# Retention and a tanh-shrink MLP on one core: who issues the transposing transfer's store, and seven products for one half block more

## The chip, the core and the metric

The kernel runs on one core of a Trainium2 chip. TensorE multiplies matrices (the profile calls it PE, and its weight loads PEld), VectorE (DVE), ScalarE (ACT) and GpSimd (POOL) work on elements, SyncE (SP) issues transfers. The metric is the device time of one launch in microseconds; before the change it is 741.86 us, the median of three runs (741.45 to 742.57). The profiled execution spans 740.2 us.

## The reference

```python
# attention: q, k, v are (4, 8, 768, 64)
gamma = 1.0 - 2.0 ** (-5.0 - np.arange(H))
for t in range(S):
    state = gamma * state + np.einsum('bhd,bhe->bhde', k[:, :, t], v[:, :, t])
    y[:, :, t] = scale * np.einsum('bhd,bhde->bhe', q[:, :, t], state)
x = y.transpose(0, 2, 1, 3).reshape(B * S, H * D)      # (3072, 512)
# MLP: w_in (512, 2048), w_out (2048, 512)
h = x @ w_in
out = (h - np.tanh(h)) @ w_out
```

## The kernel before

The 3072 rows are handled in 24 *chunks* of 128 (attention) and in 12 *half blocks* of 256 (MLP). The retention is computed chunk by chunk: scores of a chunk (masked products of k and q), plain sums of outer products of k and v (the state), and outputs. For the scores, k and q are needed transposed. The first eight chunks are transposed on TensorE, the other sixteen by a transfer: ScalarE splits the words of k and scaled q into 16-bit halves (`apart`), one transfer stores them in DRAM (`rows`), and a second, transposing transfer reads them back as `kqT`.

```python
def turn_by_dma(ci):
    apart = mid.tile([P, 2, 2, H * D], U16, tag="apart", name=f"apart_{ci}", bufs=1)
    for which in range(2):
        words = loaded[ci][which].rearrange("p h d -> p (h d)").bitcast(U16)
        nc.scalar.copy(out=apart[:, :, which],                                   # L277
                       in_=words.rearrange("p (n two) -> p two n", two=2))
    rows = dram.tile([P, 2, 2 * H * D], U16, tag="rows", name=f"rows_{ci}")
    nc.sync.dma_start(out=rows, in_=apart.rearrange("p two i n -> p two (i n)"))  # L280
    sides[ci] = mid.tile([P, 2, NP, P], F32, tag="kqT", name=f"kqT_{ci}")
    nc.sync.dma_start_transpose(                                                  # L282
        out=sides[ci].rearrange("p i n t -> p (i n) t").bitcast(U16),
        in_=rows.rearrange("p two n -> (p two) n"),
    )
```

`products(ci)` multiplies first k with v (L302, the plain sums) and then the two sides of `kqT` (L308, the scores), into the two PSUM banks with the tag "t".

The weights arrive as 64-bit floats and are converted on the chip, one tile of 128 x 512 after the other: two ScalarE operations (L176, L177), four of VectorE (L185 to L191), two of GpSimd (L199, L203). `load_weights` on SyncE's queue (L153, L158) fills one of three `raw` buffers and waits until the buffer is free.

The MLP runs in *steps*: in each, `up` makes 256 columns of h for one half block (8 matmuls of 128x256, L420), ScalarE and VectorE turn h into g = h - tanh(h), and two steps later `down` multiplies that g with the output weights. An ordinary `down` is 4 matmuls of 128x512 (L468). From half block FAST on, the 2x2 block product is done with seven products in place of eight (the Strassen-Winograd form): 7 matmuls of 128x256 (L579), for which GpSimd makes four sums of each g (L544 to L547) and, once, 16 differences of weights (L535). At the end of such a half block one ScalarE copy and seven VectorE operations put its results together.

Each matmul of the code stands as two records in the profile, so `up` is x16, an ordinary `down` x8, and seven products x14.

```python
FAST = 6
...
def fast_weights(k, at):
    if not room:
        ...                            # buffers of "raw", "head", "low", "power"
        late = xp.tile([P, 4, 2, TH], F32, tag="xT", name="fast_x")
        room.extend(late[:, i] for i in range(4))
    ...
    nc.gpsimd.tensor_tensor(t, a, b, op=ALU.subtract)                             # L535
...
def fast_banks(n):
    if not spare:
        t = banks("t", "fast_t")
        whole = y_banks.rearrange("p two r n t -> p r two n t")
        spare.append([t[:, 0], t[:, 1], whole[:, 0].rearrange("p two n t -> p (two n t)"),
                      bank("o", "fast_o"), bank("o", "fast_o")])
        spare.append(whole[:, 1].rearrange("p two n t -> p (two n t)"))
    five, sixth = spare
    first, second, third = five[:3]
    spare[0] = five[3:] + [first, second, third]
    ...
```

A half block takes three of the five banks in turn and half of the sixth. `y_banks` are the outputs' two banks, "o" those of the ordinary `down`.

The main loop, steps 8 to 95. Steps with a chunk (`ci`) are 9, 11, 13 and so on to 45; `ci` is 5 in step 9 and 20 in step 39. Half blocks 0 to 3 share the first 32 steps; half block 4 has steps 32 to 39, half block 5 steps 40 to 47, and each later one eight more.

```python
with_chunk = {BEGUN + 2 * i + 1: FIRST - 3 + i for i in range(NCH - FIRST + 3)}
with_weights = {BEGUN: [12, 13]}
for i in range(14, NW):
    with_weights[i - 5] = [i]
with_fast = {4 * NM // 2 + 1 + i: (i % 4, i // 4) for i in range(2 * PAIRS)}

for s in range(BEGUN, len(steps)):
    n, m2, first, last = steps[s]
    ci = with_chunk.get(s)
    if ci is not None:
        if ci + 3 < NCH:
            scale(ci + 3, 0, nc.gpsimd)          # q, L240
            scale(ci + 3, 1, nc.gpsimd)          # v, L240
        if ci >= FIRST:
            outputs_rest(ci)
            keep_x(ci)
        if FIRST <= ci + 2 < NCH:
            products(ci + 2)                     # L302, L308
            mask(ci + 2)
            state(ci + 2)
        load_chunk(ci + 4)                       # k, q, v, L233
        if FIRST <= ci + 1 < NCH - 1:
            outputs(ci + 1)
            see(ci + 1)
    for i in with_weights.get(s, []):
        convert(i)
        load_weights(i + 3)
    for i in range(2):
        up(n, m2, i)
    ...
    if ci is not None and ci + 3 < NCH:
        turn_by_dma(ci + 3)
    waiting.append(steps[s])
    shrink_begin(n, m2)
    shrink_factors(n, m2)
    shrink_multiply(n, m2)
    downs(LAG)                                   # LAG = 2
    shrink_end(n, m2)
    if n >= FAST:
        fast_sums(n, m2)
    if s in with_fast:
        fast_weights(*with_fast[s])
downs(0)
```

Of the kernel before, what the change touches and what calls it, by code (L numbers as in the profile page):

```python
# [32 lines left out]
def kernel(  # L33
# [24 lines left out]
    nc = tc.nc  # L58
# [6 lines left out]
    NM = DF // P  # L65
    CPB = S // P
    NCH = NT // P
# [19 lines left out]
    def bank(tag, name):  # L87
        return ps.tile([P, BANK], F32, tag=tag, name=name)

    def banks(tag, name):  # L90

        return ps.tile([P, 2, BANK], F32, tag=tag, name=name, bufs=1)
# [4 lines left out]
    at = [0]  # L97
# [22 lines left out]
    NW = 2 * NM  # L120
# [84 lines left out]
    def convert(i):  # L205
        convert_begin(i)
        convert_bits(i)
        convert_end(i, nc.gpsimd)
# [17 lines left out]
    def load_chunk(ci):  # L226
        if ci >= NCH:
            return
        b, j = divmod(ci, CPB)
        loaded[ci] = []  # L230
        for nm, src in (("k", k), ("q", q), ("v", v)):
            t = inp.tile([P, H, D], F32, tag=nm, name=f"{nm}_{ci}", bufs=4 if nm == "v" else 2)
            nc.sync.dma_start(out=t, in_=src[b, :, ts(j, P), :].rearrange("h p d -> p h d"))  # L233
            loaded[ci].append(t)

    def scale(ci, which, engine):
        if ci >= NCH:
            return
        t, g = loaded[ci][1 + which], (gq, gv)[which]
        engine.tensor_tensor(t, t, g[:, ts(ci % CPB, H)][:, :, None].to_broadcast([P, H, D]),  # L240
                             op=ALU.mult)
# [29 lines left out]
# [6 lines that stand above are left out]
            nc.scalar.copy(out=apart[:, :, which],  # L277
                           in_=words.rearrange("p (n two) -> p two n", two=2))
        rows = dram.tile([P, 2, 2 * H * D], U16, tag="rows", name=f"rows_{ci}")
        nc.sync.dma_start(out=rows, in_=apart.rearrange("p two i n -> p two (i n)"))  # L280
        sides[ci] = mid.tile([P, 2, NP, P], F32, tag="kqT", name=f"kqT_{ci}")
        nc.sync.dma_start_transpose(  # L282
            out=sides[ci].rearrange("p i n t -> p (i n) t").bitcast(U16),
            in_=rows.rearrange("p two n -> (p two) n"),
        )
# [26 lines left out]
    def mask(ci):  # L312
        halves = scores[ci]
        m = mid.tile([P, 2, NP, D], F32, tag="a", name=f"a_{ci}")
        nc.vector.tensor_tensor(m, halves[:, :, 0],
                                causal[:, None, None, :].to_broadcast([P, 2, NP, D]),
                                op=ALU.mult)
        masked[ci] = m
# [18 lines left out]
    y_banks = banks("y", "y").rearrange("p r (two n t) -> p two r n t", two=2, n=2)  # L337
# [44 lines left out]
    def see(ci):  # L382
        y = y_banks[:, ci % 2]
        for col in range(2):
            for r in range(2):
                nc.scalar.copy(out=seen[ds(D * col, D), r : r + 1],  # L386
                               in_=y[ds(D * col, D), r, 1, ds(D * ((ci + r + col) % 2), 1)])

    def outputs_rest(ci):
        halfway.pop(ci)(False)  # L390
        loaded.pop(ci)

    def keep_x(ci):
        n, nj = divmod(ci, BLK)
        if nj == 0:
            xT[n] = xp.tile([P, NP, BLK * P], F32, tag="xT", name=f"xT_{n}")

        half = xT[n][:, :, ts(nj // 2, TH)].rearrange("p (n r) t -> p r n t", r=2)
        y = y_banks[:, ci % 2][:, :: 1 - 2 * (ci % 2)]
        for odd in range(2):  # L400
            nc.scalar.copy(out=half[:, :, :, ds(P * odd + D * (nj % 2), D)],
                           in_=y[:, :, :, odd::2])
# [103 lines left out]

    FAST = 6
    PAIRS = NM // 2  # L510
    room = []
    t_of = {}
# [1 line left out]
    def quarter(i, c, at):  # L514
        return w2[:, i::2, ts(c, TH)][:, ds(2 * at, 2)]

    def fast_weights(k, at):

        if not room:
            for _ in range(3):  # L520
                raw = stage.tile([P, 2, 2, TH], F32, tag="raw", name="fast_raw", bufs=3)
                room.extend(raw[:, i] for i in range(2))
            for tag in ("head", "low", "power"):
                room.extend(stage.tile([P, 2, TH], F32, tag=tag, name=f"fast_{tag}")
                            for _ in range(2))
            late = xp.tile([P, 4, 2, TH], F32, tag="xT", name="fast_x")
            room.extend(late[:, i] for i in range(4))
        t = t_of[k, at] = room[PAIRS // 2 * k + at]
        a, b = (
            (quarter(0, 1, at), quarter(0, 0, at)),  # L530
            (quarter(1, 1, at), t_of.get((0, at))),
            (quarter(1, 1, at), quarter(0, 1, at)),
            (t_of.get((1, at)), quarter(1, 0, at)),
        )[k]
        nc.gpsimd.tensor_tensor(t, a, b, op=ALU.subtract)  # L535
# [13 lines left out]

    spare = []
    accs = {}

    def fast_banks(n):
        if not spare:
            t = banks("t", "fast_t")
            whole = y_banks.rearrange("p two r n t -> p r two n t")
            spare.append([t[:, 0], t[:, 1], whole[:, 0].rearrange("p two n t -> p (two n t)"),
                          bank("o", "fast_o"), bank("o", "fast_o")])  # L560
            spare.append(whole[:, 1].rearrange("p two n t -> p (two n t)"))
        five, sixth = spare
        first, second, third = five[:3]
        spare[0] = five[3:] + [first, second, third]
        acc = {1: first, 2: first, 5: second, 7: second, 3: third, 4: third, 6: sixth}
        right = {2: 1, 7: 1, 4: 1, 6: n % 2}
        accs[n] = {k: b[:, ts(right.get(k, 0), TH)] for k, b in acc.items()}

    def fast_down(n, m2, first, last):
        if first:  # L570
            fast_banks(n)
        left = fast_g.pop((n, m2))
        for k in (1, 2, 4, 6, 7, 5, 3):
            right = (
                w2[:, 2 * m2, :TH], w2[:, 2 * m2 + 1, :TH], w2[:, 2 * m2 + 1, TH:],
                *(t_of[x, m2 // 2][:, m2 % 2] for x in (3, 0, 1, 2)),
            )[k - 1]

            nc.tensor.matmul(accs[n][k], left[k - 1], right, start=first and k in (1, 6, 7, 4),  # L579
                             stop=last, skip_group_check=True)  # L580
# [28 lines left out]
    def downs(lag):  # L609
        while len(waiting) > lag:  # L610
            tile_ = waiting.pop(0)
            if tile_[0] >= FAST:
                fast_down(*tile_)
# [60 lines left out]


    FIRST = 8
    with_chunk = {BEGUN + 2 * i + 1: FIRST - 3 + i for i in range(NCH - FIRST + 3)}
    with_weights = {BEGUN: [12, 13]}
    for i in range(14, NW):
        with_weights[i - 5] = [i]  # L680
    with_fast = {4 * NM // 2 + 1 + i: (i % 4, i // 4) for i in range(2 * PAIRS)}

    for s in range(BEGUN, len(steps)):
        n, m2, first, last = steps[s]
        ci = with_chunk.get(s)
        if ci is not None:
            if ci + 3 < NCH:
                scale(ci + 3, 0, nc.gpsimd)
                scale(ci + 3, 1, nc.gpsimd)
            if ci >= FIRST:  # L690
                outputs_rest(ci)
                keep_x(ci)
            if FIRST <= ci + 2 < NCH:
                products(ci + 2)
                mask(ci + 2)
                state(ci + 2)
            load_chunk(ci + 4)
            if FIRST <= ci + 1 < NCH - 1:
                outputs(ci + 1)
                see(ci + 1)  # L700
# [5 lines that stand above are left out]
        if ci == NCH - 2:  # L706
            outputs(ci + 1)
            see(ci + 1)
        if ci is not None and ci + 3 < NCH:
            turn_by_dma(ci + 3)  # L710
        waiting.append(steps[s])
        shrink_begin(n, m2)
        shrink_factors(n, m2)
        shrink_multiply(n, m2)
        downs(LAG)
        shrink_end(n, m2)
        if n >= FAST:
            fast_sums(n, m2)
        if s in with_fast:
            fast_weights(*with_fast[s])  # L720
    downs(0)


# [52 lines left out]
```

## Time and profile before

| | us |
|---|---|
| median of three runs | 741.86 |
| span of the profiled execution | 740.2 |
| TensorE, `up` (L420), 1536 records | 351.6 |
| TensorE, ordinary `down` (L468), 384 records | 173.0 |
| TensorE waiting for `kqT` before L308 | 3.44, once |
| store `rows<-apart`, issue to landing, least / median / most | 2.9 / 3.8 / 5.4 |
| transposing transfer `kqT<-rows`, issue to landing, the same | 4.1 / 4.2 / 4.7 |

The page gives the busy time of each engine, the chain of work that ended last, the costliest groups of instructions and the transfers. In a list of waits a line names who waited, for what, how long in all, how often and the longest. In a timeline a line has the start, the duration, the engine, the line of the kernel, the operation with its output and inputs, the count, and in brackets the idle time before it with what ended it. The duration of a matmul record reaches beyond the start of the next, as matmuls are pipelined; what a group costs is read from start to start. "Granted clock" is the share of TensorE's full clock.

### The profile page before, as it was taken

How to read it: one execution, taken by the hardware profiler on the slowest of the kernel's cores; microseconds unless marked ns; L12 is line 12 of the kernel's file. 1: busy time of each engine (PE TensorE's matmuls, PEld its weight loads, DVE VectorE, ACT ScalarE, POOL GpSimd, SP SyncE). 2: the span in 40 equal slices, each digit the busy share in tenths (PEclk: the TensorE clock that was granted, in tenths of full speed). 3: DMA queues.
4: the chain of work that ended last, by engine and by line, in shares of the span. 5: the costliest groups of instructions: out<-in, count | busy, mean ns of one | idle time of the engine just before them, and what ended most of it. 6: DMA issues, size and time to landing. Idle time of an engine off the chain costs nothing.

```text
span 740.2 us, 14746 instructions
## 1 busy us (share of the span) xinstructions
PE 723.9 (98%) x5758; PEld 560.5 (76%) x5758; DVE 532.3 (72%) x843; ACT 390.0 (53%) x749; POOL 231.0 (31%) x316
## 2 busy tenths in 40 slices
PE   8899998999999999999999999999999999999996
PEld 7686665676677667667666688888888888888885
DVE  4989988898889767666455666676676766766764
ACT  4477565766767654655453444444444444444441
POOL 0565435444454412227000032222222232222221
PEclk9999999999999999999999999999999999999999
DMA  9863428676766556544200000000000000000000
GB/s 205 220 186 86 129 71 195 166 196 168 184 182 158 138 131 167 147 100 101 59 30 1 0 30 0 2 29 1 0 29 1 29 2 1 28 1 1 29 1 28
DMA packets 125396, 59.81 MB, mean 81 GB/s; under 512 B 109840, under 2 KB 118160, under 8 KB 125328
## 3 DMA queue, kind: packets, MB, share of 16 engines
q1 hardware_dynamic: 125184, 58.73, 30.8%
q8 instruction: 45, 0.74, 0.4%
q10 hardware_dynamic: 144, 0.15, 0.1%
q14 instruction: 23, 0.19, 0.1%
HBM read 35.80 MB, written 14.68 MB: 68 GB/s over the span
## 4 chain that ended last, share of the span: by engine, by line
PE 95%; DMA 2%; DVE 1%; SPq 1%; ACT 0%; issue 0%; DVEq 0%; ACTq 0%
PE h L420 45%; PE o L468 22%; PE fast_t L579 7%; PE y L579 6%; PE fast_o L579 6%; PE y L356 3%; PE s L302 1%; PE s L308 1%; PE kqTp L254 1%; PE kqTp L216 1%; DMA raw<-in_moe_w_in_dram 1%; DMA k<-in_k_dram 1%; SPq L233 1%; DMA kqT<-rows 1%; SPq L158 0%; DVE power L191 0%
## 5 line engine op out<-in xcount | busy, mean ns | idle before, releaser
L420 PE MATMUL h<-xT,w 128*128 128x256 f32 x1536 | 351.6, 382 | 1.1 <-DVE w L203 1.1
L420 PEld LDWEIGHTS h<-xT,w 128*128 128x128 f32 x1536 | 290.9, 191 | 53.1 <-issue 12.9
L429 ACT ACTIVATE u<-h 128x512 f32<-128x512 f32 x96 | 57.3, 597 | 269.4 <-PE h L420 269.1
L445 DVE TENSOR_TENSOR th<-h,th 128x512 f32<-128x512 f32 x96 | 66.2, 690 | 149.7 <-ACT th L430 149.7
L468 PE MATMUL o<-w,g 128*128 128x512 f32 x384 | 173.0, 593 | 0.0
L468 PEld LDWEIGHTS o<-w,g 128*128 128x128 f32 x384 | 72.6, 190 | 71.4 <-issue 67.9
L544 POOL TENSOR_TENSOR s<-g 128x128 f32<-128x128 f32 x48 | 21.8, 454 | 292.2 <-DVE g L459 214.3
L459 DVE COPY_PREDICATED g<-large,th 128x512 f32<-128x512 int32 x96 | 73.7, 768 | 10.2 <-DVE g L458 0.9
L448 DVE SCALAR_TENSOR_TENSOR h<-q,h 128x512 f32<-128x512 f32 x96 | 66.8, 696 | 10.4 <-DVE h L446 0.5
L454 DVE SCALAR_TENSOR_TENSOR h<-q,h 128x512 f32<-128x512 f32 x96 | 66.6, 694 | 8.6 <-DVE h L448 0.5
L199 POOL TENSOR_TENSOR low<-low,power 128x512 f32<-128x512 f32 x30 | 38.4, 1280 | 108.8 <-DVE power L191 75.2
L458 DVE TENSOR_TENSOR g<-h,u 128x512 f32<-128x512 f32 x96 | 66.3, 691 | 6.4
L437 ACT ACTIVATE q<-u,tab 128x512 f32<-128x512 f32 x96 | 69.4, 723 | 0.0
L438 ACT ACTIVATE q<-u,tab 128x512 f32<-128x512 f32 x96 | 69.1, 720 | 0.0
L439 ACT ACTIVATE large<-u,tab 128x512 f32<-128x512 f32 x96 | 68.7, 716 | 0.0
L446 DVE SCALAR_TENSOR_TENSOR h<-u,h 128x512 f32<-128x512 f32 x96 | 65.8, 685 | 0.0
L430 ACT ACTIVATE th<-h 128x512 f32<-128x512 f32 x96 | 56.8, 592 | 0.0
L240 POOL TENSOR_TENSOR q<-q,tab 128x512 f32<-128x512 f32 x22 | 24.0, 1090 | 94.0 <-DMA q<-in_q_dram 74.7
L203 POOL TENSOR_TENSOR w<-low,head 128x512 f32<-128x512 f32 x30 | 38.6, 1285 | 2.4
L356 PEld LDWEIGHTS y<-a,v 64*64 64x64 f32 x768 | 15.9, 134 | 15.3 <-ACT large L439 11.4
L240 POOL TENSOR_TENSOR v<-v,tab 128x512 f32<-128x512 f32 x22 | 27.1, 1231 | 0.1
L386 ACT COPY seen<-y 64x1 f32<-64x1 f32 x96 | 10.1, 154 | 28.3 <-PE y L356 27.9
(110 smaller groups left out, 820.8 us busy)
## 6 DMA issues: line engine op xcount, KB each, us to landing
rows<-apart SPq DMA_DIRECT2D x16, 512.0 KB, 3.8
k<-in_k_dram SPq DMA_DIRECT2D x24, 256.0 KB, 4.2
q<-in_q_dram SPq DMA_DIRECT2D x24, 256.0 KB, 4.8
v<-in_v_dram SPq DMA_DIRECT2D x24, 256.0 KB, 5.1
raw<-in_moe_w_out_dram SPq DMA_DIRECT2D x12, 512.0 KB, 4.2
out_dram<-sum SPq DMA_DIRECT2D x24, 256.0 KB, 2.3
raw<-in_moe_w_in_dram SPq DMA_DIRECT2D x14, 256.0 KB, 4.2
raw<-in_moe_w_in_dram SPq DMA_DIRECT2D x28, 128.0 KB, 4.1
```

Of the source, the lines that this page charges most:

```text
L420: nc.tensor.matmul(hp, w1[:, c, ts(2 * m2 + i, P)], xT[n // 2][:, c, ts(n % 2, TH)], start=(i == 0 and c == 0), stop=(c == NC - 1), skip_g ...
L437: nc.scalar.activation(q0, u, AF.Square, bias=bias0)
L438: nc.scalar.activation(q1, u, AF.Square, bias=bias1, scale=math.sqrt(A))
L439: nc.scalar.activation(large, u, AF.Relu, bias=bias_m)
L445: nc.vector.tensor_tensor(th, hp, th, op=ALU.subtract)
L446: nc.vector.scalar_tensor_tensor(hp, in0=u, scalar=R, in1=hp, op0=ALU.subtract, op1=ALU.mult, reverse0=True)
L448: nc.vector.scalar_tensor_tensor(hp, in0=q0, scalar=C0, in1=hp, op0=ALU.add, op1=ALU.mult)
L454: nc.vector.scalar_tensor_tensor(hp, in0=q1, scalar=A * C1, in1=hp, op0=ALU.add, op1=ALU.mult)
L458: nc.vector.tensor_tensor(flat, hp, u, op=ALU.mult)
L459: nc.vector.copy_predicated(flat, large.bitcast(I32), th)
L468: nc.tensor.matmul(o_p[j], gT[n, m2][:, i, ts(j, P)], w2[:, 2 * m2 + i], start=(first and i == 0), stop=(last and i == 1))
L579: nc.tensor.matmul(accs[n][k], left[k - 1], right, start=first and k in (1, 6, 7, 4), stop=last, skip_group_check=True)
```

## The change

The store of `apart` goes from SyncE's queue to ScalarE's, so that it needn't queue behind SyncE's other transfers. The scaling of a chunk's q and v is written at the end of the step before, and `turn_by_dma` ahead of the weights' conversion and loads and ahead of `up` instead of after it. FAST becomes 5, so that half block 5 gets its seven products too. As the outputs' banks are still in use when it starts, the order of the banks changes: the scores' two banks and one "o" bank come first, the other "o" bank is the sixth. The weights' differences are made two in a step from step 28 on instead of one in a step from step 33, and those that need the late buffer come last.

```diff
-        nc.sync.dma_start(out=rows, in_=apart.rearrange("p two i n -> p two (i n)"))
+        nc.scalar.dma_start(out=rows, in_=apart.rearrange("p two i n -> p two (i n)"))
...
-    FAST = 6
+    FAST = 5
...
+        if k == 3 and at == 0:
             late = xp.tile([P, 4, 2, TH], F32, tag="xT", name="fast_x")
...
-            whole = y_banks.rearrange("p two r n t -> p r two n t")
-            spare.append([t[:, 0], t[:, 1], whole[:, 0].rearrange("p two n t -> p (two n t)"),
-                          bank("o", "fast_o"), bank("o", "fast_o")])
-            spare.append(whole[:, 1].rearrange("p two n t -> p (two n t)"))
+            whole = y_banks.rearrange("p two r n t -> p r (two n t)")
+            o = [bank("o", "fast_o") for _ in range(2)]
+            spare.append([t[:, 0], t[:, 1], o[0], whole[:, 0], whole[:, 1]])
+            spare.append(o[1])
...
+    LAST_WEIGHTS = NW - 6
...
-    with_fast = {4 * NM // 2 + 1 + i: (i % 4, i // 4) for i in range(2 * PAIRS)}
+    fast_parts = [(k, at) for at in range(PAIRS // 2) for k in range(3)]
+    fast_parts += [(3, at) for at in range(PAIRS // 2)]
...
-            if ci + 3 < NCH:
-                scale(ci + 3, 0, nc.gpsimd)
-                scale(ci + 3, 1, nc.gpsimd)
...
             load_chunk(ci + 4)
+            if ci + 3 < NCH:
+                turn_by_dma(ci + 3)
...
-        if ci is not None and ci + 3 < NCH:
-            turn_by_dma(ci + 3)
...
-        if s in with_fast:
-            fast_weights(*with_fast[s])
+        if s + 1 in with_chunk:
+            for which in range(2):
+                scale(with_chunk[s + 1] + 3, which, nc.gpsimd)
+        if s > LAST_WEIGHTS + 1:
+            for _ in range(min(2, len(fast_parts))):
+                fast_weights(*fast_parts.pop(0))
```

## The prediction

> **What bounds the kernel now.** I read the page from the top: busy times first, then the chain that ended last.
>
> ```profile
> PE 723.9 (98%) x5758; PEld 560.5 (76%) x5758; DVE 532.3 (72%) x843; ACT 390.0 (53%) x749; POOL 231.0 (31%) x316
> ...
> PE 95%; DMA 2%; DVE 1%; SPq 1%; ACT 0%; issue 0%; DVEq 0%; ACTq 0%
> ```
>
> TensorE (PE) holds 95% of the chain. So only two kinds of gain exist: less work on TensorE, or a hole in its work closed. The idle times of the other engines cost nothing by themselves.
>
> Next, the list of waits (columns: engine and line that waited, what it waited for, total us, times, longest us). The largest of TensorE's own is this one:
>
> ```profile
> PE s L308 <- DMA kqT<-rows: 3.4, 1, 3.4
> ```
>
> It happens once. The timeline of TensorE around it (start us, duration us, engine, line, operation, count) shows where:
>
> ```profile
> 119.26 0.69 PE L302 MATMUL s<-v,k 64*64 64x64 f32 x32
> 123.40 0.69 PE L308 MATMUL s<-kqT 64*64 64x64 f32 x32 [3.44 <-DMA kqT<-rows]
> 124.02 5.41 PE L420 MATMUL h<-xT,w 128*128 128x256 f32 x16
> ```
>
> This is step 11 of the main loop, the scores of chunk 8, the first chunk turned by a transfer. Its plain sums (L302) run at 119.26, and then TensorE waits until 123.40 for `kqT`. The third line is the hidden half of the cost: the 16 up-projection matmuls that follow take 5.34 us from start to start in the chain of waits in order of time, where every other such group takes 3.45. The table by stretches says why (columns from the left: stretch, length, busy of PE, PEld, DVE, ACT, POOL, then the granted clock):
>
> ```profile
> 112.45:115.90 3.45, 3.45 (x17) 3.04 (x17) 3.28 (x6) 3.06 (x6) 1.78 (x2) 1.00 0.66 158
> 124.02:127.60 3.58, 3.58 (x15) 2.93 (x10) 3.44 (x8) 1.04 (x1) 1.44 (x1) 0.55 1.21 218
> ```
>
> The clock after the hole is 0.55, before it 1.00. So the hole costs 3.44 + (5.34 - 3.45) = 5.33 us.
>
> After 140 us TensorE never waits again: with chunks two steps take 16.06 us throughout (starts at 141.54, 157.60, 173.66 in the chain), without chunks one step takes this:
>
> ```profile
> 402.59:409.48 6.89, 6.89 (x26) 4.56 (x25) 4.12 (x6) 2.91 (x5) 0.00 (x0) 1.00 0.01 2
> 409.48:416.36 6.88, 6.88 (x25) 4.56 (x24) 4.13 (x6) 2.91 (x5) 0.00 (x0) 1.00 0.00 0
> 436.61:443.09 6.48, 6.48 (x32) 5.70 (x31) 4.13 (x7) 2.92 (x6) 1.74 (x4) 1.00 0.01 3
> 443.09:449.56 6.47, 6.47 (x31) 5.70 (x30) 4.12 (x7) 2.90 (x6) 1.73 (x4) 1.00 0.00 0
> ```
>
> The first two are steps with the ordinary down-projection, the last two with seven products. TensorE is full in all four; VectorE, ScalarE and GpSimd have over 2 us to spare.
>
> Why is the transfer late? The issues on SyncE's queue, then ScalarE's copies:
>
> ```profile
> 113.50 1.68 SPq L158 DMA_DIRECT2D raw<-in_moe_w_in_dram  x3
> 115.28 0.54 SPq L280 DMA_DIRECT2D rows<-apart  x1
> 119.07 1.95 SPq L282 DMA_TRANSPOSE kqT<-rows  x1
> ```
>
> ```profile
> 110.52 1.05 ACT L277 COPY apart<-q 128x1024 uint16<-128x1024 uint16 x1 [2.59 <-POOL q L240]
> ```
>
> `apart` is complete at 111.57, but the store goes out at 115.28, because SyncE first has to issue weight loads that wait for a free `raw` buffer (VectorE's L189 at 112.74). The store lands 3.79 us later, when the transposing transfer starts; that lands 4.28 us later, at 123.35.
>
> **What the Trainium skill says.** "DMA: Bandwidth & Descriptors", section "Anatomy of one DMA — SWDGE (gpsimd) path": transfers don't wait on semaphores, the issuing sequencer does, before dispatch. The trace agrees: 3.71 us from 111.57 to 115.28 behind another transfer's wait. The same page, "Issuing engines are not separate DMA queues": starting transfers from several engines saves only the sequencer's time. So I credit the move with that 3.71 us and not with faster landing; no run yet shows a ScalarE store here. "TensorE: Matmul & The Clock Gate", section "What's actually happening": an idle window of about 3.4 us halves the clock. The trace shows 0.55 after a hole of 3.44 us. "SBUF — State Buffer", section "SBUF: two separate sides": VectorE and GpSimd share a port pair, and one fully blocks the other. I read L187's 1.39 us at 103.19, beside GpSimd's L199 and L203, against its usual 0.43, as that.
>
> **The change part by part.**
>
> (a) *Seven products for half block 5.* Eight steps lose 4 matmuls of 128x512 (8 records) and gain 7 of 128x256 (14 records). From the table: (6.89 + 6.88)/2 = 6.885 us against (6.48 + 6.47)/2 = 6.475. That is 0.41 a step, **3.3 us** for eight. It lies wholly on the path, as TensorE is full there. Beside it GpSimd gets 32 more sums of 0.455 us (14.6 us) in steps 40 to 47, where it is idle (73.4 us idle before 425.72). VectorE gets 7 combining operations of about 0.42 us instead of one copy of 0.69; half blocks 6 to 11 do the same without TensorE waiting.
>
> (b) *Banks.* Half block 5 starts in step 42, when the outputs' banks are in use until step 45. The new order gives it the scores' two banks and two `o` banks, last read in step 41; `up` of step 42 (3.45 us) lies between. I count 0.
>
> (c) *The 16 weight differences two per step from step 28.* Each takes 1.27 to 1.52 us, so 2.5 to 3 us of GpSimd in a step of 6.9 to 9.2. Before, the last was computed at 427.49, too late for half block 5, which starts at about 376. Count: 0.
>
> (d) *The store on ScalarE, and the order.* On GpSimd the scaling keeps its place behind the weights of the step before and ahead of its own step's, so it isn't really sooner for chunk 8: q is scaled at 109.45 either way. The copy of q ends at 111.57, and I start the store at 111.65. Its landing took 2.9 to 5.4 us; with three loads just ahead (issued 108.11 to 111.15) I take 4.5, so 116.15. SyncE is free, as the weight loads now come after. Plus 4.28: `kqT` lands at 120.4, against a need at 119.95. The hole shrinks from 3.44 to about 0.5 us. That should leave the clock alone: early in the kernel a wait of 1.05 us (before 25.12) kept it at 1.00, while one of 2.17 us (before 31.31) was followed by 0.50. Gain 5.33 - 0.5 = **4.8 us**.
>
> (e) *What it delays.* ScalarE now does both copies (2.1 us) and an issue (I take 0.4, SyncE's median) ahead of the two conversion operations (1.4 us) and the activations. In step 9 these start near 113.4 instead of 111.47. VectorE's chain then runs about 1.1 us later, and so do weight tile 15 (done 122.98 before, now near 124.2; needed at 124.8) and chunk 9's scaling. I work chunk 9 on: copy of q done at 126.2, store landed at 130.8, turned at 135.1; TensorE wants it at about 135.3, since it is early by 5 us. Both fit with tenths to spare. I charge **0.3 us**.
>
> (f) The 15 later stores gain some microseconds each, but TensorE doesn't wait for them: 0.
>
> Sum: 3.3 + 4.8 - 0.3 = 7.8 us; 741.86 - 7.8 = 734.0.
>
> **The rivals.**
>
> *The hole moves.* Closing it makes step 13 come 5 us sooner, while GpSimd and VectorE, which feed chunk 9 and weight 15, don't speed up. For it: the margins of (e). Against it: VectorE catches up about 1 us a step after that. A new wait of 1 to 2 us gives 735 to 736; one of over 2 us, which may halve the clock again, 737 to 739.
>
> *The transfers are hidden anyway and the rest is noise.* Then only (a) counts: 738.5. Against it stands the 3.44 us hole with its releaser.
>
> *ScalarE becomes the bound, by waiting in its stream for GpSimd and issuing.* It waits 269.1 us for `up` over the span, and is at 53%. It would show only in steps 9 to 15. No net loss is plausible from 16 issues of 0.4 us.
>
> *Half block 5 waits for its sums or banks.* A wait of 1 us in each of its eight steps would turn -3.3 into +4.7, so 742. The seven-product steps of half block 6 show none.
>
> **Range and chances.** Everything closed gives 741.86 - 3.3 - 5.33 = 733.2, so little lies below 732.5. Above lie the moved hole and a landing over 5 us. 8 in 10: 732.5 to 737.5. Two per cent is 14.8 us, nearly twice the largest gain I can find, and no rival loses that much: faster 0.01, same 0.98, slower 0.01.
>
> **What would show it.** (a): steps of half block 5 at 6.48 us, 112 more L579 records. (d): the store on ScalarE's queue near 111.7, transposing transfer near 116, the wait at L308 under 1 us, clock 1.00 after it, next `up` group 3.45 us. (e): no wait of TensorE on `w` or on `kqT` in steps 11 and 13. The prediction fails if the store from ScalarE lands much later than 4.5 us, if issuing blocks ScalarE for microseconds, or if a wait over 3 us appears after the first is closed.

## The result and the profile after

The changed kernel takes 733.89 us (median of four runs, 732.94 to 734.36) against 742.22 before (741.45 to 742.93): a ratio of 0.9886, 95% interval 0.9869 to 0.9904, so 8.3 us. A second series gave 733.45 against 742.15, ratio 0.989 (0.9875 to 0.9905).

The page after has the same shape. These are its busy times and the chain of waits by engine:

```profile
PE 717.7 (98%) x5806; PEld 566.9 (77%) x5806; DVE 533.6 (73%) x849; ACT 389.7 (53%) x749; POOL 247.6 (34%) x348
...
PE 91%; DMA 4%; DVE 2%; POOL 1%; SPq 1%; ACT 1%; issue 0%; DVEq 0%; POOLq 0%; ACTq 0%
```

TensorE is still the bound. Its share of the chain fell from 95% to 91%, and transfers rose from 2% to 4%: the chain now runs through the transposing transfers of chunks 8 and 9. In the list of waits, the one that the prediction began with has shrunk, but it occurs twice:

```profile
PE s L308 <- DMA kqT<-rows: 0.9, 2, 0.6
```

TensorE's timeline in steps 11 and 13 (start, duration, line, operation, count) shows both:

```profile
118.22 0.69 PE L302 MATMUL s<-v,k 64*64 64x64 f32 x32
119.25 0.69 PE L308 MATMUL s<-kqT 64*64 64x64 f32 x32 [0.33 <-DMA kqT<-rows]
119.87 3.72 PE L420 MATMUL h<-xT,w 128*128 128x256 f32 x16
123.43 3.60 PE L468 MATMUL o<-w,g 128*128 128x512 f32 x8
...
133.84 0.69 PE L302 MATMUL s<-v,k 64*64 64x64 f32 x32
135.13 0.69 PE L308 MATMUL s<-kqT 64*64 64x64 f32 x32 [0.60 <-DMA kqT<-rows]
```

The 3.44 us of chunk 8 are now 0.33, and chunk 9, which did not wait before, waits 0.60. From 119.87 to 123.43 the group of `up` takes 3.56 us, not the 5.25 of before (124.02 to 129.27). The clock in that stretch, and a step of half block 5, in the table by stretches (stretch, length, five busy times, then the granted clock):

```profile
119.87:123.43 3.56, 3.56 (x23) 3.15 (x17) 3.32 (x6) 0.04 (x1) 3.02 (x3) 1.00 0.71 208
395.92:402.39 6.47, 6.47 (x31) 5.70 (x30) 4.11 (x7) 2.91 (x6) 1.74 (x4) 1.00 0.00 0
```

The clock is 1.00, and the step takes 6.47 us where an ordinary one took 6.885.

The transfer that closed the hole, in the order of time (the second line is ScalarE's queue, the last two are SyncE's):

```profile
109.49 1.05 ACT L277 COPY apart<-q 128x1024 uint16<-128x1024 uint16 x1 [4.52 <-POOL q L240]
110.57 0.35 ACTq L280 DMA_DIRECT2D rows<-apart  x1
...
114.89 2.10 SPq L282 DMA_TRANSPOSE kqT<-rows  x1
...
117.11 4.36 SPq L158 DMA_DIRECT2D raw<-in_moe_w_in_dram  x6
```

The store follows the copy by 0.03 us, and the weight loads, six at once, come after the transposing transfer. ScalarE waits 4.52 us for the scaling ahead of its copy of q.

TensorE's timeline allows a full account: it is cut at the first `up` matmul of chosen steps, from one trace per kernel. All lengths are in us. Between steps 13 and 42, and from 50 to 95, all fourteen traces agree within 0.02, but for one: the run with the filled hole took 231.59 from 13 to 42.

| kernel | steps 9 to 11 | 11 to 13 | 13 to 42 | 42 to 50 | 50 to 95 | 9 to 95 |
|---|---|---|---|---|---|---|
| before | 18.62 | 17.45 | 231.34 | 57.33 | 291.37 | 616.11 |
| changed | 15.51 | 16.59 | 231.33 | 54.03 | 291.38 | 608.84 |
| changed, again | 15.59 | 16.49 | 231.34 | 54.04 | 291.37 | 608.83 |
| e1, products only | 18.68 | 17.44 | 231.34 | 54.03 | 291.37 | 612.86 |
| e2, transfer part only | 15.50 | 16.40 | 231.34 | 57.32 | 291.38 | 611.94 |
| e3, store on ScalarE only | 15.75 | 15.76 | 231.33 | 57.32 | 291.38 | 611.54 |
| e4, order only | 15.28 | 16.34 | 231.33 | 57.33 | 291.37 | 611.65 |
| e5, hole filled | 18.65 | 15.76 | 231.59 | 57.32 | 291.38 | 614.70 |
| e6, scaled before conversion | 14.96 | 15.76 | 231.34 | 54.03 | 291.38 | 607.47 |
| e7, products, store on ScalarE | 15.73 | 15.76 | 231.34 | 54.04 | 291.37 | 608.24 |
| e8, only chunk 8 on ScalarE | 15.82 | 17.41 | 231.34 | 57.33 | 291.37 | 613.27 |
| e11, only scaled sooner | 18.12 | 17.31 | 231.35 | 57.32 | 291.38 | 615.48 |
| e12, scaled sooner, SyncE | 15.56 | 16.55 | 231.33 | 54.04 | 291.37 | 608.85 |

(The repetition of e6 gave 14.96, 15.76, 231.33, 54.04, 291.37 and 607.46.) Steps 9 to 11 without any wait take 14.96, steps 11 to 13 take 15.76. So before, the hole cost 18.62 - 14.96 = 3.66 and the slow clock 17.45 - 15.76 = 1.69. In the changed kernel 0.55 and 0.83 of that are left. The gain from step 9 to 95 is 3.11 + 0.86 + 3.30 = 7.27 us.

### The profile page after: what moved, and what is told of

It reads as the page before. It is cut to its first block, busy times and chain, and to the rows that moved or that the text cites. A ratio compares the mean times of both kernels' runs of the same rounds, so it can differ in the third digit from the quotient of the medians.

```text
span 731.9 us, 14885 instructions
## 1 busy us (share of the span) xinstructions
PE 717.7 (98%) x5806; PEld 566.9 (77%) x5806; DVE 533.6 (73%) x849; ACT 389.7 (53%) x749; POOL 247.6 (34%) x348
## 4 chain that ended last, share of the span: by engine, by line
PE 91%; DMA 4%; DVE 2%; POOL 1%; SPq 1%; ACT 1%; issue 0%; DVEq 0%; POOLq 0%; ACTq 0%
PE h L420 44%; PE o L468 17%; PE fast_t L581 8%; PE y L581 8%; PE fast_o L581 7%; PE y L356 3%; DMA kqT<-rows 1%; PE s L302 1%; PE s L308 1%; DMA raws<-in_moe_w_in_dram 1%; DMA k<-in_k_dram 1%; DMA q<-in_q_dram 1%; SPq L233 1%; PE kqTp L254 1%; DMA rows<-apart 1%; DVE head L189 0%
## 5 line engine op out<-in xcount | busy, mean ns | idle before, releaser
L468 PE MATMUL o<-w,g 128*128 128x512 f32 x320 | 144.2, 593 | 0.0
L545 POOL TENSOR_TENSOR s<-g 128x128 f32<-128x128 f32 x56 | 25.5, 455 | 286.7 <-DVE g L459 282.3
L468 PEld LDWEIGHTS o<-w,g 128*128 128x128 f32 x320 | 60.5, 190 | 59.5 <-issue 56.7
L356 PEld LDWEIGHTS y<-a,v 64*64 64x64 f32 x768 | 15.9, 134 | 14.9 <-ACT large L439 10.9
L546 POOL TENSOR_TENSOR s<-s,g 128x128 f32<-128x128 f32 x56 | 25.6, 457 | 4.4
```

The source lines that it names most:

```text
L468: nc.tensor.matmul(o_p[j], gT[n, m2][:, i, ts(j, P)], w2[:, 2 * m2 + i], start=(first and i == 0), stop=(last and i == 1))
```

## The experiments

My theory was that two parts add up: seven products worth 0.41 us a step for eight steps, and a late store of chunk 8 that cost a wait and, behind it, a halved clock. The rivals were that only one of the two counted, that the clock was no part of it, or that ScalarE's queue as such was what helped.

**e1, the products alone.** The changed kernel with its transfer part undone:

```diff
-        nc.scalar.dma_start(out=rows, in_=apart.rearrange("p two i n -> p two (i n)"))
+        nc.sync.dma_start(out=rows, in_=apart.rearrange("p two i n -> p two (i n)"))
# scale(...) and turn_by_dma(...) back to their places in the kernel before
```

> The seven products for half block 5 with the new banks and the earlier weight differences, but the store on SyncE, the scaling and the turning where they were. My theory (the two parts add up, products worth 8 x 0.41 = 3.3 us, wholly on the path): 742.2 - 3.3 = 738.9, the wait of 3.4 us at L308 in step 11 still there, steps of half block 5 at 6.48 us. Rival (banks or sums make half block 5 wait, and the transfer part brought more than its hole): 740 to 742. Rival (the products brought nearly all): 734 to 735.

Measured: 738.67 us against 741.78, ratio 0.9957 (0.9945 to 0.9969). Only the column 42 to 50 of the table differs from before, by 3.30 us; the wait at L308 is 3.49. So nothing of the new banks or the earlier differences shows in the steps. The end is 1.24 us longer than before (19.95 us from step 95 on, against 18.71): the last output transfer took 3.5 us from issue to landing where it took 2.3 before. Why is not shown.

**e2, the transfer part alone.** The changed kernel with `FAST = 6`.

> The whole change but FAST stays 6, so half block 5 keeps its ordinary down-projection. My theory: the hole and the halved clock behind it are gone (5.3 us), some 0.5 to 1 us comes back as waits in steps 11 and 13: 737.0 to 737.7. If the parts add up, the gain of this run and of the run with the products alone sum to the 8.3 us of the change within 0.8. Rival (only the wait itself, 3.4 less the new waits, was won and the clock is no part of it): 739.5 to 740.

Measured: 737.35 us, ratio 0.994 (0.9926 to 0.9954). The gains of e1 and e2, 3.1 and 4.4 us, sum to 7.5, within 0.8 of the 8.3. The rival that leaves the clock out, 739.5 or more, falls.

**e3, the store alone, and e4, the order alone.** Both start from the kernel before:

```diff
# e3
-        nc.sync.dma_start(out=rows, in_=apart.rearrange("p two i n -> p two (i n)"))
+        nc.scalar.dma_start(out=rows, in_=apart.rearrange("p two i n -> p two (i n)"))
# e4: scale(...) at the end of the step before, turn_by_dma(...) ahead of the
#     conversion and of up, as in the change; the store stays on nc.sync
```

> The kernel before with one edit: the store issued by ScalarE. Everything else as it was. Theory A (the store waited only behind SyncE's weight loads, so either its move to ScalarE or the new order suffices for chunk 8): store near 111.7, wait in step 11 under 1 us, time 737 to 738, the same as with the whole transfer part. Theory B (both parts of it are needed, since SyncE's transposing issue still stands behind the weight loads): the wait stays over 2 us and the time is 740 to 742.

> The kernel before with the order alone: scaling written at the end of the step before, turning ahead of the conversion and of up; the store stays on SyncE. Theory A (either edit suffices): the store goes out near 111.7 on SyncE's queue, ahead of the weight loads, wait in step 11 under 1 us, 737 to 738. Theory B (ScalarE's queue is what matters): the wait in step 11 stays over 2 us, 740 to 742.

Measured: e3 736.57 us, ratio 0.9932 (0.992 to 0.9944); e4 736.94, ratio 0.9933 (0.9921 to 0.9946). Both lie a little below the 737 to 738 of theory A, whose mechanism they show: the two edits can stand in for each other. Either lets the store of chunk 8 pass the weight loads. In e3 it does so from another queue (first block, e3), in e4 by standing ahead of them in the same queue (second block, e4):

```profile
111.34 0.34 ACTq L280 DMA_DIRECT2D rows<-apart  x1
...
113.24 1.69 SPq L158 DMA_DIRECT2D raw<-in_moe_w_in_dram  x3
115.61 2.29 SPq L282 DMA_TRANSPOSE kqT<-rows  x1
```

```profile
110.49 0.61 SPq L280 DMA_DIRECT2D rows<-apart  x1
114.68 2.00 SPq L282 DMA_TRANSPOSE kqT<-rows  x1
```

In both, the transposing transfer starts 4.2 to 4.3 us after the store. In e3 the weight loads go out between the two, and the wait in step 11 is still only 0.56 us. By the table, e3 gains 4.57 us from step 9 to 95, e4 4.46, both together (e2) 4.17. With the new order TensorE waits for chunk 9 in e4 (0.35 us) and in the changed kernel (0.60), with the store alone (e3) it does not. In e2 chunk 9 came in time as well; the 0.64 us that its steps 11 to 13 lose are one pause between matmuls of L356, at 135.41 to 136.13, for which the profile shows no releaser.

**e5, the hole filled.** The kernel before, with 13 multiplications of zeros between the two halves of chunk 8's products:

```diff
+        if ci == 8:
+            idle[0] = 13
+            keep_busy(sp[:, 0, :P])
         for p in range(NP):        # the scores, L308 before
```

> The kernel before, with 13 more multiplications of zeros (128x128, results overwritten) between the plain sums and the scores of chunk 8: TensorE is busy in most of the 3.4 us, yet must still wait until kqT has landed. Theory (the halved clock after the hole is a cost of its own, 1.9 us): clock 1.00 after the wait, next up group 3.45 us from start to start instead of 5.34, time 739.5 to 740.3. Rival (the clock's dip costs nothing in the end, or comes from something else than the idle time): 741.5 to 742, or the dip still there.

TensorE's timeline (the scores are at L311 here, `up` at L423), and the stretch of the `up` group:

```profile
118.93 3.17 PE L216 MATMUL s<-busy 128*128 128x128 f32 x26
122.45 0.69 PE L311 MATMUL s<-kqT 64*64 64x64 f32 x32 [0.36 <-DMA kqT<-rows]
123.08 3.72 PE L423 MATMUL h<-xT,w 128*128 128x256 f32 x16
```

```profile
123.08:126.63 3.55, 3.55 (x21) 3.14 (x17) 3.41 (x8) 1.04 (x1) 1.44 (x1) 1.00 1.01 226
```

The scores start no sooner than before (18.65 us for steps 9 to 11), but the clock stays at 1.00 and steps 11 to 13 take 15.76 us instead of 17.45. This shows the clock as a cost of its own, 1.69 us. Nor is it an accident of one trace: all three traces in which TensorE stands still for 2.84 us or more at this place (before, e1, e11) have the slow stretch behind it, and none of the other eleven has one there. The time is 740.77 us, ratio 0.9983 (0.9975 to 0.999): 1.3 us gained, less than the 1.8 to 2.6 I had expected. The spans fell by 2.0 (medians 738.05 and 740.1); the device time lies 2.9 us above the span here and 2.0 in the kernel before, for a reason that the runs do not show.

**e7, the products with the store alone.** e1 with the store on ScalarE.

> The products for half block 5 and the store on ScalarE, but the scaling and the turning in the order of before. Theory (the new order brings nothing once the store is on ScalarE): 741.8 - 5.2 - 3.1 = 733.5, within 0.6 of the changed kernel. Rival (the order matters once half block 5 is fast too): 735 or more.

Measured: 734.67 us, ratio 0.9904 (0.9892 to 0.9917); between the two expectations, and so inconclusive as a time. Its trace from step 9 to 95 is the sum of e1 and e3: 608.24, 0.6 us less than the changed kernel. Its span ends 7.6 us after the start of the last product, the changed kernel's 6.6. Up to the issue of the last output transfer the two ends are alike; this transfer then takes 3.3 us to land instead of 2.3, as in e1, and why is not shown. That the new order brings nothing is shown for the steps, not for the time.

**e8, only chunk 8's store on ScalarE.** The kernel before with one line changed:

```diff
-        nc.sync.dma_start(out=rows, in_=apart.rearrange("p two i n -> p two (i n)"))
+        (nc.scalar if ci == 8 else nc.sync).dma_start(out=rows, in_=apart.rearrange("p two i n -> p two (i n)"))
```

> The kernel before, with the store issued by ScalarE for chunk 8 alone; the fifteen later ones stay on SyncE. Theory (only chunk 8's transfer was on the path): 736.5 to 737.5, as with all sixteen on ScalarE. Rival (once the first hole is closed, step 13 comes 5 us sooner and finds chunk 9's transfer late): a new wait of over 1 us at L308 in step 13, 738 to 741.

Measured: 738.32 us, ratio 0.9956 (0.9942 to 0.9969). The rival was right: the hole moved to chunk 9. TensorE's two waits, then SyncE's queue ahead of the second:

```profile
119.42 0.69 PE L308 MATMUL s<-kqT 64*64 64x64 f32 x32 [0.63 <-DMA kqT<-rows]
...
136.13 0.69 PE L308 MATMUL s<-kqT 64*64 64x64 f32 x32 [1.43 <-DMA kqT<-rows]
```

```profile
126.37 1.68 SPq L158 DMA_DIRECT2D raw<-in_moe_w_in_dram  x3
128.15 0.54 SPq L280 DMA_DIRECT2D rows<-apart  x1
131.91 1.34 SPq L282 DMA_TRANSPOSE kqT<-rows  x1
```

Chunk 9's copy of q ended at 123.91 and its store went out at 128.15, behind weight loads again. The steps 11 to 13 take 17.41 us against 15.76 in e3: chunk 9's store is worth 1.65. From step 13 on the two agree, so the other fourteen stores are worth nothing.

**e6, the scaling really a step sooner.** In the change, the scaling still stands on GpSimd behind the weight tile of the step before. Here it goes ahead of that tile, for all chunks:

```diff
+        if s + 1 in with_chunk:
+            for which in range(2):
+                scale(with_chunk[s + 1] + 3, which, nc.gpsimd)
         for i in with_weights.get(s, []):
             convert(i)
...
-        if s + 1 in with_chunk:
-            for which in range(2):
-                scale(with_chunk[s + 1] + 3, which, nc.gpsimd)
```

> The changed kernel, with the scaling really a step sooner: on GpSimd it now stands ahead of the weight tiles of the step before, not behind them. Theory (the rest of the wait at L308, 0.9 us in the changed kernel, hangs on GpSimd's order, as ScalarE's copy of q waits for the scaling): chunk 8 turned some 4 us sooner, no wait for kqT, 732.6 to 733.3. Rival (the scaling's 2.3 us push the weight tiles back, and TensorE waits for those instead): a wait on w at L468 in steps 10 to 12, 734 to 736.

> The kernel with the scaling ahead of the weight tiles of the step before, again, side by side with the changed one. Its trace had no wait for kqT and was 1.1 us ahead of the changed kernel from step 9 on (0.33 and 0.60 us of waits and what follows them). So 0.9 to 1.5 us less than the changed kernel: 732.4 to 733.5. If the earlier gain was chance, the two are equal within 0.5.

> The changed kernel once more, beside the one with the scaling ahead of the conversion. From step 9 on its trace was 7.3 us ahead of the kernel before, and 1.0 us more was there before step 9, where the two programs are the same. If that 1.0 us is chance: 7.3 to 8.0 us below the kernel before, so 734.0 to 734.8. If it belongs to the change: 733.4 to 733.9, and the profile again reaches step 9 a microsecond sooner.

Measured: 732.47 us, ratio 0.9878 (0.9862 to 0.9895), and in the repetition 732.62 against 733.45 of the changed kernel beside it. ScalarE and the queues in steps 8 and 9 of e6:

```profile
104.25 1.05 ACT L277 COPY apart<-q 128x1024 uint16<-128x1024 uint16 x1
...
105.33 0.37 ACTq L280 DMA_DIRECT2D rows<-apart  x1
...
110.57 3.18 SPq L282 DMA_TRANSPOSE kqT<-rows  x1
```

The copy no longer waits for GpSimd, the transposing transfer starts 6.83 us after the beginning of step 9 (103.74) instead of 10.53 in the changed kernel (104.36), and the list of waits has no `kqT` on TensorE. Both traces of e6 are 1.37 us ahead of the changed kernel's from step 9 to 95. Of that, 0.29 us goes again behind step 95, where e6 takes 19.00 us and the changed kernel 18.71. The medians of the pair differ by 0.83, short of the 0.9 to 1.5 expected, and their ranges overlap; the gain is shown in the traces, less firmly in the times. It is the fastest version of the study.

**e11 and e12, the sooner scaling without the other edits.** e11 is the kernel before with only the scaling moved ahead of the previous step's tile; e12 is e6 with the store back on SyncE.

> The kernel before with one edit: the scaling on GpSimd ahead of the weight tiles of the step before; store on SyncE and turning where they were. Theory (any of three edits takes chunk 8's store off its late start): the copy of q no longer waits for the scaling, ends near 108, the store still stands behind the weight loads and goes out near 111 to 113, wait in step 11 under 1 us: 736.3 to 737.5. Rival (behind the weight loads it stays late whatever the scaling does): wait over 2 us, 740 or more.

> The changed kernel with the scaling ahead of the conversion, but the store back on SyncE. Theory (with the turning ahead of the weight loads the issuing engine doesn't matter): no wait for kqT over 0.5 us, 732.4 to 733.6, equal to the same kernel with ScalarE's store within 0.5. Rival (ScalarE's queue lets the store pass the loads of k, q and v): store lands later, waits of 1 us or more, 734 to 735.

e11 measured 740.25 us, ratio 0.9978 (0.9967 to 0.9988). My theory of it failed. SyncE's queue, then TensorE:

```profile
111.97 1.68 SPq L158 DMA_DIRECT2D raw<-in_moe_w_in_dram  x3
...
113.75 0.54 SPq L280 DMA_DIRECT2D rows<-apart  x1
...
117.74 2.00 SPq L282 DMA_TRANSPOSE kqT<-rows  x1
```

```profile
122.13 0.79 PE L308 MATMUL s<-kqT 64*64 64x64 f32 x32 [2.84 <-DMA kqT<-rows]
122.84 5.27 PE L420 MATMUL h<-xT,w 128*128 128x256 f32 x16
```

The copy ended at 108.20, counted from the start of step 9 2.7 us sooner than before, yet the store left at 113.75, behind the weight loads. While the queue was closed, this readiness took only 0.60 us off the wait. And 2.84 us of waiting were again followed by a slow `up`.

e12 measured 733.39 us, ratio 0.9887 (0.9873 to 0.99). That lies in the range of the theory, but 0.77 us above the same kernel with ScalarE's store beside it, where 0.5 was allowed; by the traces it is 1.38 us from step 9 to 95. Its waits at L308 are those of the changed kernel, 0.37 and 0.56. Here the store stands behind the loads of k, q and v, which wait too:

```profile
107.23 0.54 SPq L233 DMA_DIRECT2D k<-in_k_dram  x1
107.87 0.53 SPq L233 DMA_DIRECT2D q<-in_q_dram  x1
108.44 1.95 SPq L233 DMA_DIRECT2D v<-in_v_dram  x1
110.49 1.02 SPq L280 DMA_DIRECT2D rows<-apart  x1
```

The copy of q had ended at 106.07. So the issuing engine does matter once the data is early enough: ScalarE's store in e6 left 0.03 us after its copy.

## Why the prediction was right, and where it was not

The steps behind the prediction held up singly, with two exceptions, (e) and (f). That the time came within 0.1 us (733.9 against 734.0) is partly luck. The sum (a) to (f) was 7.8 us and measured 7.27, from step 9 to 95. Another 1.04 us, in front of step 9, which no part of the prediction claims, brought the gain to 8.3, and the kernel before took 0.36 us more beside the changed one than the prediction started from (742.22 for 741.86), which hid most of the excess.

- **(a) Products: 3.3 us.** Measured 3.30 (57.33 to 54.03), in e1 and in the changed kernel alike. **(b) and (c), banks and differences: 0.** e1 shows no other difference.
- **(d) The store: hole from 3.44 to 0.5 us, and no slow clock.** Measured 0.33 and 1.00. The changed kernel's trace reached step 9 at 104.36 instead of 105.40; with that 1.04 taken off, the start I gave for the store (111.65) is 110.61, measured 110.57. The landing, taken as 4.5, was 4.32, slower than the 3.79 of SyncE's store before, so the move brought no faster landing. I credited the engine's change with the time behind SyncE's weight loads and nothing else; e3 and e4 show that this is what it was worth here. That the scaling would not be sooner is also so: q is scaled at 108.41, which is 109.45 less 1.04. The 5.33 us that I gave the hole are right by two errors that cancel: by the table the wait cost 3.66, not 3.44, and the slow clock 1.69, not 1.89. I had compared the slow group of 5.34 us with groups of 3.45, but in the same chain a group that follows a chunk's products takes 3.65 (start, then us):

```profile
141.54 3.65 PE h L420 x16
```

- **(e) Delays: charged 0.3 us, measured 0.83** in steps 11 to 13. This term of the sum was mis-sized, and its sign, no wait for `kqT` in steps 11 and 13, did not come: there are two. ScalarE's delay was as worked out (activations of step 9 at 112.16; predicted 113.4 less 1.04), weight tile 15 was in time (122.96), and chunk 9's copy of q started at 123.99. Its transposing transfer, however, took 6.02 us where I had put 4.28, and that made the wait of 0.60. With 4.28 it would have landed at 133.35, ahead of the scores. The repetition (5.91) and e4 (6.08) show the same. Three weight loads were issued 2 to 3.5 us after its start, before only one; but beside the same three it took 4.33 in e2 and 4.45 in e12, so why it took longer stays open.
- **(f) The fifteen later stores: 0.** Wrong for one of them. e8 shows that chunk 9's store is worth 1.65 us once chunk 8's hole is closed. I had worked out chunk 9's time with its store on ScalarE, but drawn no conclusion for the case without. The rival "the hole moves" was thus real, and the change met most of it by moving all the stores.

About 1 us of the 8.3 stays outside this account. From step 9 to 95 the gain is 7.27, and from step 95 on both traces take 18.71 us. The other 1.04 us lie in front of step 9, where the change leaves the program as it was: the trace before reached it at 105.40, the changed one at 104.36. They arise near 31 us. In the trace before, TensorE waited 2.17 us there (until 31.31) and the clock then was 0.50 from 32.24 to 35.66; in the changed one it waited 1.83 us (until 30.95) and the clock stayed at 1.00. The repetition (e9) met what I had expected if this microsecond belonged to the change, 733.4 to 733.9 and step 9 sooner: 733.45 and 104.01. Yet the other eleven traces, five of them with the order of before, reach step 9 between 103.74 and 105.15 as well, so it is the trace before that was late. Chance need not be all of it, as the spans of e11 (median 738.5 of 21 runs) lie 1.7 us below those of the kernel before (740.2 of 25), and its steps 9 to 95 are only 0.63 us shorter. This stays open.

## What to carry to other kernels

SyncE's queue issued its transfers here in the order of the code. So a store that was ready waited for the loads ahead of it: of the 3.71 us, 1.93 went by until their buffer was free (113.50), and 1.78 in issuing three of them. Move such a store to another queue or ahead of those loads, and check that its data is not itself late. When a hole on the bounding engine is closed, work out the same chain for the next one at the pace of the kernel without the hole. And read a hole on TensorE together with the matmuls behind it, as the slow clock can add half as much again.

## What the hardware showed beyond expectation

- A wait of TensorE costs more than its record, as this counts from the modelled end of the matmuls before it. Without a wait the scores start 0.51 us after the plain sums (139.68 to 140.19 before); in step 13 of the changed kernel they started 1.29 us after them (133.84 to 135.13). So 0.78 us were lost where the record has 0.60, close to the 0.83 of the table.
- ScalarE issues the store in 0.34 us at the median, where SyncE took 0.38, and its next activation starts 0.4 to 0.5 us after the copy ends; sixteen of these issues do not show in TensorE's steps from 13 to 42.
- The length of one wait does not tell whether the clock will be halved. In steps 9 to 13, waits of 1.43 us (e8) and less left it at 1.00, while those of 2.84 us (e11) and 3.44 us (before) were followed by 3.41 us at 0.50 (from 124.40 in the kernel before). Half of 3.41 us fits the measured cost of 1.69. But early in e3 a wait of 2.53 us (until 31.74) left the clock at 1.00, as the stretch below shows, and in e12 it was 0.50 from 17.38 to 20.79 after waits of only 1.03 us (until 14.91) and 0.74 us (until 16.09). So no limit between 1.05 and 2.17 us, as (d) took it from two early waits, decides here, nor does an unbroken idle window of about 3.4 us, which the prediction quotes. What does, these runs do not show.

```profile
31.74:35.20 3.46, 3.46 (x70) 3.24 (x70) 3.14 (x5) 1.63 (x3) 1.88 (x2) 1.00 0.85 211
```
